# Second MLP weights prepared on GpSimd during the attention and kept in DRAM; sums of the first MLP weights on GpSimd; second-matmul tiles one product later

## The chip, the core and the metric

The kernel runs on one core of one Trainium2 chip. The metric is the time of one execution on the device in microseconds (us). Before the change it is 2522.59 us (median of three runs, 2522.47 to 2524.62).

Five things run side by side, each with a queue of its own that is worked off strictly in order: PE (TensorE, matmuls), DVE (VectorE), ACT (ScalarE), POOL (GpSimd) and SP (here only the issuer of DMA transfers). An instruction at the head of a queue that waits for another engine holds up all that stands behind it.

## The reference

One transformer block over 2048 tokens of width 576 in float32: attention with 32 heads of width 18 that share one key and value head, then a channel MLP of width 4608, both with modulated layer norms.

```
mod = (silu(c) @ w_mod) -> sa, ca, ga, sb, cb, gb
h = layernorm(x) * (1 + ca) + sa
x = x + ga * attention(h)                     # softmax, one k and v head for 32 q heads
h = layernorm(x) * (1 + cb) + sb
y = layernorm(h)                              # the MLP's own norm
x = x + gb * (gelu(y @ w1 + b1) @ w2 + b2)    # w1: 576x4608, w2: 4608x576
```

## The kernel before

**Precision.** Most large matmuls take operands in a rounded float32 form that PE reads in one pass. To keep accuracy an operand is split into a rounded part ("hi", written by ACT with a rounding copy) and a remainder ("lo", the difference, written by DVE or POOL), and a product of two operands is the three matmuls hi*hi, hi*lo and lo*hi.

**Three stages.** The first stage normalises the input and makes q, k and v. The second is the attention: 32 steps n (one per group of heads and block of 512 tokens), each with 16 inner steps kc. Between them `between` (L785) puts work of other kinds into the queues: `posts` finish a group of heads, and at every odd kc `step(fill)` takes one more piece of a generator (L803): output projection, the second layer norm of the first two token blocks (`ln2_tile`, L516, whose multiply and add are on POOL for these blocks), and at the last n `first_split` (L694), which splits the first group of first-MLP weights.

**The MLP stage** (L834 to L1067) is a loop over 36 steps v: two halves of 1024 tokens, 18 groups of 256 hidden columns. A step multiplies the normalised input, two blocks of 512 tokens by two column halves, with the group's first weights. It uses seven products (`product`, L909) in place of eight: sums and differences of input pieces (`op_pieces`) and of weight pieces (`w1_sum`, S1 to S4) are multiplied and the results combined. I call the products P1 to P7 in their order in the loop: three of six matmuls and four of eight. After P4, P5, P6 and P7 a 128-partition result of 512 columns goes through `gelu` (L924). I call these four gelus g00, g11, g10 and g01 after the f and b in the code. Each is a chain: two ACT operations on the result in PSUM (L931, L932), DVE (L934), ACT tanh (L935), DVE (L937), ACT hi (L938), POOL lo (L939). Its work buffer `gx` has two copies.

The result of step v goes into the second matmul, `fc2` (L941), which is a generator of eight tiles, T1 to T8 here, each 12 matmuls of 288 columns and one DVE addition into the residual `XT` (L958). These tiles run in step v+1, one per call of `t_()`, between the products. Their PSUM tile `psA` has two buffers, so a tile can start only after the DVE addition of the tile two before it.

**Weights.** The first weights of step v+1 are split during step v. The raw group (`w1r`, 640 KB) is loaded once per step into one buffer (L646, at the end of the step, issued by SP when the last reader of the old group is done). `w1_sum` (L665) makes a sum on DVE, ACT writes its hi (L649), and `w1_sum_lo` (L681) writes its lo on DVE (L652); single pieces have their lo on POOL (`w1_a`, `w1_22`, `w1_tails`). The second weights of a group (two pieces of 128x576) are loaded raw (L900) in every step, scaled with the gate `BC[:, 2]` on POOL (L905), rounded on ACT (L906) and their lo made on POOL (L907): `w2_split`. This happens twice per group, once for each half of the tokens.

**What else runs in the loop.** `more()` puts one piece of a generator at seven places of each step. In v = 1 to 9 this is the second layer norm of the last two token blocks, one tile of 128 tokens per step, with multiply and add on DVE (L534, L535). In v = 17 it forms the input pieces for the second half (`op_pieces`). I call the other steps (v = 10 to 16 and 18 to 34) the plain steps.

**Between attention and MLP** (L862 to L888) the input pieces of the first half are formed on ACT, DVE and POOL while PE ends the last output projection.

Of the kernel before, what the change touches and what calls it, by code (L numbers as in the profile page):

```python
# [8 lines left out]
F32 = mybir.dt.float32  # L9
# [23 lines left out]
def block_kernel(ctx: ExitStack, tc, x, wqkv, wo, w1, b1, w2, b2, c, wmod, ident_in, out):  # L33
# [31 lines left out]

    qscr = dr.tile([NB, 2, H * DH, TB], F32, name="qscr")
# [449 lines left out]
    def ln2_tile(tb, t):  # L516
# [17 lines left out]
        e.tensor_mul(h, h, BC[:, 1, :])  # L534
        e.tensor_tensor(h, h, BC[:, 0, :], op=ALU.add)  # L535
# [101 lines left out]
    def w1_rooms():  # L637
        W1["a"] = px.tile([128, KD, 2, 128], F32, name="w1r")
        W1["s"] = px.tile([128, 2, 128], F32, name="w1s")
        W1["d"] = px.tile([128, 128], F32, name="w1d")  # L640
# [24 lines left out]
    def w1_sum(a):  # L665

        o = W1["s"]
        def op(x, y, how):
            ve.tensor_tensor(o, x, y, op=how)  # L669
# [11 lines left out]
    def w1_sum_lo(a):  # L681
        w1_lo(a, 2, W1["s"], ve)

    def w1_tails(e=po):
# [3 lines left out]
        ve.tensor_tensor(d, t[:, 0], t[:, 1], op=ALU.subtract)  # L688
        ac.activation(W1["r"][:, 16], d, AF.Copy)
        for o, i in ((slice(14, 16), t), (16, d)):  # L690
            h = W1["r"][64:, o]
            e.tensor_tensor(h, i[64:], h.bitcast(F32), op=ALU.subtract)

    def first_split():  # L694
# [5 lines left out]
        w1_sum(4)  # L700
        w1_a()
        w1_sum_lo(4)
        yield
        w1_sum(6)
        w1_22()
        w1_sum_lo(6)
        yield
        w1_sum(10)
        w1_sum_lo(10)
        yield  # L710
        w1_sum(12)
        w1_sum_lo(12)
# [72 lines left out]
    def between(n, kc):  # L785
# [16 lines left out]
        if kc % 2:  # L802
            step(fill)  # L803

# [34 lines left out]
    def op_pieces(R):  # L839


        at = {"B11": (0, 0, ve), "B21": (2, 2, po), "B22": (4, 7, po), "T2": (6, 5, ve), "T1": (8, 5, ve),
              "T3": (10, 0, ve), "T4": (12, 2, ve), "t0": (0, 4, po), "t1": (1, 9, po)}
# [18 lines left out]
    form = op_pieces(YR[0])  # L862
# [5 lines left out]
    todo = deque(("+B11 +T2", "-B11 =T3 +B21 +T3", "-T2 -B21", "-T3"))  # L868
# [11 lines left out]
    form("+t0 -t0 =T4 =T1 +T1 +T4 +t1 -t1")  # L880
# [4 lines left out]
    form("-T1 -T4 +B22 -B22")  # L885
# [5 lines left out]
    W2R = [px.tile([128, D], F32, name="w2r", bufs=2) for _ in range(2)]  # L891
# [6 lines left out]
    def load_w2(v):  # L898
        for f in range(2):
            sy.dma_start(W2R[f], w2[v % NG, :, f, :])  # L900

    def w2_split(v, f, e):

        (h, l), o = W2[v % 2], W2R[f]
        e.tensor_tensor(o, o, BC[:, 2, :], op=ALU.mult)  # L905
        ac.activation(h[:, f], o, AF.Copy)  # L906
        e.tensor_tensor(l[:, f], o, h[:, f].bitcast(F32), op=ALU.subtract)  # L907
# [68 lines left out]
    load_w2(0)  # L976
    for v in range(NV):
        nx = v + 1 < NV
        e2 = po if v else ve
# [128 lines left out]
```

## Time and profile before

| what | value |
|---|---|
| median of three runs | 2522.59 us |
| profiled execution, its own time | 2520.07 us |
| its span, first to last instruction | 2518.3 us |
| mean granted PE clock | 0.987 |
| busy share PE, DVE, ACT, POOL | 93%, 83%, 71%, 36% |
| first MLP product starts at | 1447.24 us |

How to read it. The page gives busy time of each engine over the whole span, and in 40 equal slices a digit for the busy tenths. The windows view gives the same for stretches that one names. The groups view (lines) gives for each line, operation and shape the count, the busy time and the mean time of one. In the timeline a row is start, duration, engine, line, operation, output and inputs, and in brackets how long the engine had been idle before and what ended that. The chain of waits goes back from the last instruction to whatever released each step. PE's busy time contains the filling of its pipeline, so a busy PE isn't yet PE at its peak. A row "PE ... x12" that follows an idle time begins a tile.

### The profile page before, as it was taken

How to read it: one execution, taken by the hardware profiler on the slowest of the kernel's cores; microseconds unless marked ns; L12 is line 12 of the kernel's file. 1: busy time of each engine (PE TensorE's matmuls, PEld its weight loads, DVE VectorE, ACT ScalarE, POOL GpSimd, SP SyncE). 2: the span in 40 equal slices, each digit the busy share in tenths (PEclk: the TensorE clock that was granted, in tenths of full speed). 3: DMA queues.
4: the chain of work that ended last, by engine and by line, in shares of the span. 5: the costliest groups of instructions: out<-in, count | busy, mean ns of one | idle time of the engine just before them, and what ended most of it. 6: DMA issues, size and time to landing. Idle time of an engine off the chain costs nothing.

```text
span 2518.3 us, 43839 instructions
## 1 busy us (share of the span) xinstructions
PE 2351.6 (93%) x16586; PEld 1468.0 (58%) x16586; DVE 2080.7 (83%) x3644; ACT 1791.9 (71%) x3512; POOL 902.6 (36%) x860
## 2 busy tenths in 40 slices
PE   8999999999999999999999978888899798899898
PEld 6644444444444544445444467777788687788777
DVE  6689999889999899997999378877777777777776
ACT  5479999889999799997999844444545555545553
POOL 6513111132410233310110145555555555555554
PEclk9999999999999999999999989999999899999999
DMA  6421000000000000000000011111111121111111
GB/s 214 132 79 41 21 22 21 16 23 21 18 21 13 20 18 21 18 21 13 21 24 12 17 53 44 39 39 40 41 51 45 45 73 45 48 44 47 43 51 48
DMA packets 48229, 102.20 MB, mean 41 GB/s; under 512 B 6683, under 2 KB 10395, under 8 KB 48017
## 3 DMA queue, kind: packets, MB, share of 16 engines
q1 hardware_dynamic: 48017, 99.39, 12.9%
q8 instruction: 131, 2.15, 0.4%
q14 instruction: 81, 0.66, 0.1%
HBM read 76.32 MB, written 14.16 MB: 36 GB/s over the span
## 4 chain that ended last, share of the span: by engine, by line
PE 52%; ACT 15%; DVE 14%; POOL 10%; issue 7%; DMA 1%; SPq 0%; DVEq 0%; POOLq 0%; ACTq 0%
PE psC L750 19%; PE psB L761 10%; PE psM L312 9%; POOL w2r L905 4%; PE psB L771 4%; DVE gx L937 3%; ACT P L763 3%; DVE w1s L669 2%; ACT psB L935 2%; PE psB L241 2%; PE psA L954 2%; ACT gx L931 2%; PE psB L584 2%; ACT psB L932 2%; POOL big L939 2%
## 5 line engine op out<-in xcount | busy, mean ns | idle before, releaser
L763 ACT ACTIVATE P<-psB 128x512 f32<-128x512 f32 x2048 | 1050.6, 621 | 1.5 <-PE psB L761 0.6
L783 DVE TENSOR_REDUCE mx<-psM 128x1 f32<-128x512 f32 x1476 | 943.5, 683 | 56.2 <-PE psM L312 29.6
L954 PE MATMUL psA<-w2s,big 128*128 128x288 f32 x2880 | 529.8, 304 | 113.4 <-DVE XT L958 86.5
L750 PE MATMUL psC<-P,V 128*32 128x256 f32 (+1 forms) x6056 | 598.0, 466 | 13.0 <-ACT O L603 13.0
L761 PE MATMUL psB<-qst,KS 64*128 64x512 f32 x2048 | 598.2, 433 | 0.5 <-DMA qst<-ms 0.4
L312 PE MATMUL psM<-KS,qst 64*128 64x512 f32 x1722 | 594.4, 431 | 2.1 <-DVE mx L783 2.1
L954 PEld LDWEIGHTS psA<-w2s,big 128*128 128x128 f32 x2880 | 445.9, 193 | 160.3 <-DVE XT L958 56.5
L919 PE MATMUL psB<-ops,w1a 128*128 128x512 f32 x1512 | 401.6, 402 | 8.4 <-DVE psB L1029 5.1
L761 PEld LDWEIGHTS psB<-qst,KS 64*128 64x128 f32 x2048 | 305.3, 184 | 168.4 <-issue 72.5
L312 PEld LDWEIGHTS psM<-KS,qst 64*128 64x128 f32 x1722 | 284.0, 184 | 121.8 <-DVE mx L781 82.5
L939 POOL TENSOR_TENSOR big<-gx,big 128x512 fp32r<-128x512 f32 x144 | 194.9, 1354 | 332.9 <-ACT big L938 198.9
L919 PEld LDWEIGHTS psB<-ops,w1a 128*128 128x128 f32 x1512 | 276.2, 192 | 57.9 <-DVE psB L1029 5.7
L750 PEld LDWEIGHTS psC<-P,V 128*32 128x32 f32 x6056 | 119.6, 108 | 231.2 <-issue 207.6
L958 DVE TENSOR_TENSOR XT<-psA,XT 128x576 f32<-128x576 f32 x288 | 212.4, 748 | 26.7 <-PE psA L954 26.6
L774 ACT ACTIVATE xc<-psB 128x512 f32<-128x512 f32 x246 | 148.2, 602 | 90.4 <-PE psM L312 75.3
L938 ACT ACTIVATE big<-gx 128x512 fp32r<-128x512 f32 x144 | 90.9, 631 | 160.1 <-DVE gx L937 160.1
L354 POOL CAST ms<-mf 16x128 fp32r<-16x128 f32 x32 | 9.0, 282 | 542.8 <-ACT mf L353 542.8
L906 ACT ACTIVATE w2s<-w2r 128x576 fp32r<-128x576 f32 x72 | 49.4, 686 | 205.1 <-POOL w2r L905 200.3
L652 DVE TENSOR_TENSOR w1a<-w1s,w1a 128x256 fp32r<-128x256 f32 x144 | 103.2, 717 | 100.2 <-ACT w1a L649 88.7
L954 PE MATMUL psA<-w1a,big 128*128 128x288 f32 x576 | 171.5, 298 | 0.0
L781 DVE CUSTOM_DVE_ANT_0 xc<-psM,xc 128x512 f32<-128x512 f32 x246 | 167.3, 680 | 0.0
L935 ACT ACTIVATE psB<-gs 128x512 f32<-128x512 f32 x144 | 86.1, 598 | 109.4 <-DVE gs L934 109.4
(167 smaller groups left out, 2810.4 us busy)
## 6 DMA issues: line engine op xcount, KB each, us to landing
w1r<-in_w SPq DMA_DIRECT2D x36, 640.0 KB
w2r<-in_w SPq DMA_DIRECT2D x72, 288.0 KB
qst<-qscr SPq DMA_DIRECT2D x192, 72.0 KB
qscr<-qs SPq DMA_DIRECT2D x16, 504.0 KB
big<-os SPq DMA_DIRECT2D x112, 72.0 KB
bigw<-in_wmod SPq DMA_DIRECT2D x5, 1440.0 KB
out<-XT SPq DMA_DIRECT2D x16, 288.0 KB
XT<-in_x SPq DMA_DIRECT2D x3, 1152.0 KB
```

What stands on the lines that cost most here:

```text
L312: pe.matmul(o, QST[n][64 * g:64 * g + 64, p, 128 * qt:128 * (qt + 1)], KS[64 * g:64 * g + 64, 512 * kb:512 * (kb + 1)], start=True, stop=True)
L750: pe.matmul(PVt[n][32 * j:32 * (j + 1), cs], V[:, kc, :], t[:, j, cs], start=(kc == 0 and h0 == 0), stop=(kc == 15), skip_group_check=True)
L761: pe.matmul(t, KS[64 * g:64 * g + 64, 128 * kc:128 * (kc + 1)], QST[n][64 * g:64 * g + 64, i, :], start=True, stop=True)
L763: ac.activation(P[n, kc][:, 2 * i + g, :], t, AF.Exp, scale=SCALE)
L774: ac.activation(XC[-1], t, AF.Relu)
L781: ve.tensor_tensor_reduce(c, t, c, 1.0, -3.0e38, ALU.add, ALU.max, o)
L783: ve.tensor_reduce(o, t, axis=AX.X, op=ALU.max)
L919: pe.matmul(o, x, y, start=(first and i == 0), stop=(i == len(terms) - 1), skip_group_check=True)
L935: ac.activation(p, s, AF.Tanh, scale=GC * GA3)
L939: po.tensor_tensor(GT[:, 2 * u + 1], h, GT[:, 2 * u].bitcast(F32), op=ALU.subtract)
L954: pe.matmul(p[:, nn, :288], x, y, start=(q == 0), stop=(q == len(terms) - 1))
L958: ve.tensor_tensor(Xv, p[:, :, :288], Xv, op=ALU.add)
```

## The change

Four edits, all quoted in the diff below.

1. **Second weights in the attention.** A generator `w2_parts` runs in the attention from n = 3 on, one piece at every odd kc after `step(fill)`. For each of the 36 pieces of 128x576 it loads the raw weights (SP), scales them, rounds them and makes the lo (three POOL operations), and stores hi and lo in DRAM (`w2scr`). Four pieces of the generator make one weight piece, so two weight pieces fall on one n, and it ends at n = 20. Its tiles share the buffers `w1s` and `w1r` that `first_split` uses later. In the MLP `w2_split` is gone, and `load_w2` brings hi and lo ready from DRAM, two transfers of 576 KB per step, at the start of step v, where raw transfers of 288 KB came in the middle of the step before.
2. **Sums on GpSimd.** In the MLP `w1_sum`, `w1_sum_lo` and the difference in `w1_tails` go to POOL; in `first_split` the sums stay on DVE. The multiply and add of `ln2_tile` are on POOL for all four token blocks.
3. **Second-matmul tiles one product later.** T1 comes after P2 (in v = 1 after P3), T2 after P3, T3 after P4, T4 after P5, T5 and T6 after P6, T7 and T8 after P7.
4. **Input pieces at the start.** Of the pieces of the first half, the lo parts of B21, B22, t0 and t1 go from POOL to DVE; T4 and T1 are formed after the last additions of the output projection; the lo parts of T1, t1, T4 and B22 are made inside step v = 0.

```
+    w2scr = dr.tile([NG, 128, 2, 2, D], F32, name="w2scr")
...
-        e.tensor_mul(h, h, BC[:, 1, :])
-        e.tensor_tensor(h, h, BC[:, 0, :], op=ALU.add)
+        po.tensor_mul(h, h, BC[:, 1, :])
+        po.tensor_tensor(h, h, BC[:, 0, :], op=ALU.add)
...
-    def w1_sum(a):
+    def w1_sum(a, e=po):
...
-            ve.tensor_tensor(o, x, y, op=how)
+            e.tensor_tensor(o, x, y, op=how)
...
-    def w1_sum_lo(a):
-        w1_lo(a, 2, W1["s"], ve)
+    def w1_sum_lo(a, e=po):
+        w1_lo(a, 2, W1["s"], e)
...
-        ve.tensor_tensor(d, t[:, 0], t[:, 1], op=ALU.subtract)
+        e.tensor_tensor(d, t[:, 0], t[:, 1], op=ALU.subtract)
...
+    def w2_parts():
+
+        for g in range(NG):
+            for f in range(2):
+                o = px.tile([128, D], F32, name="w2o", tag="w1s")
+                sy.dma_start(o, w2[g, :, f, :])
+                yield
+                po.tensor_tensor(o, o, BC[:, 2, :], op=ALU.mult)
+                yield
+                hl = px.tile([128, 2, D], F32R, name="w2p", tag="w1r")
+                po.tensor_copy(hl[:, 0], o)
+                yield
+                po.tensor_tensor(hl[:, 1], o, hl[:, 0].bitcast(F32), op=ALU.subtract)
+                sy.dma_start(w2scr[g, :, :, f, :], hl.bitcast(F32))
+                yield
...
         if kc % 2:
             step(fill)
+            if n > 2:
+                step(prep)
...
-    todo = deque(("+B11 +T2", "-B11 =T3 +B21 +T3", "-T2 -B21", "-T3"))
+    todo = deque(("+B11 +T2", "-B11 =T3 +B21 +T3", "-T2 -T3", "-B21"))
...
-    form("+t0 -t0 =T4 =T1 +T1 +T4 +t1 -t1")
+    form("+t0 -t0")
...
-    form("-T1 -T4 +B22 -B22")
+    form("=T4 =T1 +T1 +t1 +T4 +B22")
...
     def load_w2(v):
-        for f in range(2):
-            sy.dma_start(W2R[f], w2[v % NG, :, f, :])
-
-    def w2_split(v, f, e):
-
-        (h, l), o = W2[v % 2], W2R[f]
-        e.tensor_tensor(o, o, BC[:, 2, :], op=ALU.mult)
-        ac.activation(h[:, f], o, AF.Copy)
-        e.tensor_tensor(l[:, f], o, h[:, f].bitcast(F32), op=ALU.subtract)
+        for l in range(2):
+            sy.dma_start(W2[v % 2][l].bitcast(F32), w2scr[v % NG, :, l])
...
+        load_w2(v)
         ba = psB()
         product(ba, 0, 0)
         ac.activation(U[:, 0], ba, AF.Copy)
-        t_()
         g_()
...
-        t_()
-        g_()
-        w2_split(v, 0, e2)
+        if v != 1:
+            t_()
+        g_()
...
-        more("-T2 =T3")
+        more("-T2 =T3", "-T1 -t1")
         t_()
+        if v == 1:
+            t_()
...
-        w2_split(v, 1, e2)
         if nx:
             w1_sum_lo(6)
-            load_w2(v + 1)
...
         g_()
+        t_()
         product(bd, 12, 4, False, (2, 1))
```

The next two excerpts of the instruction order show a plain step. First POOL before the change, one step from the lo of g10 on (`big<-gx`, the gelu's lo). L692 are the tail pieces of the first weights, L905 and L907 the scaling and the lo of the second weights, L652 the lo of single first-weight pieces.

```order
L939 TENSOR_TENSOR big<-gx,big 128x512
L692 TENSOR_TENSOR w1a<-w1r,w1a 64x256
L692 TENSOR_TENSOR w1a<-w1d,w1a 64x128
L939 TENSOR_TENSOR big<-gx,big 128x512
L905 TENSOR_TENSOR w2r<-w2r,BC 128x576
L907 TENSOR_TENSOR w2s<-w2r,w2s 128x576
L652 TENSOR_TENSOR w1a<-w1r,w1a 128x512
```

The same place on POOL after it, again from the lo of g10 on: L672 are the additions that make a sum, L691 the difference of the tails, L695 the tail pieces (L692 before), L655 the lo of sums and of pieces, L954 the gelu's lo.

```order
L954 TENSOR_TENSOR big<-gx,big 128x512
L672 TENSOR_TENSOR w1s<-w1r,w1a 128x256
L672 TENSOR_TENSOR w1s<-w1s,w1a 128x256
L691 TENSOR_TENSOR w1s<-w1r 128x128
L695 TENSOR_TENSOR w1a<-w1r,w1a 64x256
L695 TENSOR_TENSOR w1a<-w1s,w1a 64x128
L655 TENSOR_TENSOR w1a<-w1s,w1a 128x256
L954 TENSOR_TENSOR big<-gx,big 128x512
L672 TENSOR_TENSOR w1s<-w1r 128x256
L672 TENSOR_TENSOR w1s<-w1s,w1r 128x256
L655 TENSOR_TENSOR w1a<-w1s,w1a 128x256
L655 TENSOR_TENSOR w1a<-w1r,w1a 128x512
```

The scaling and lo of the second weights are gone from this queue. In their place stand the additions of S4 and, behind the lo of g01, those of S2, whose first operand is the freshly loaded `w1r`.

On DVE before, the end of a step and the start of the next one (L1051 is the addition behind P7, L958 the addition of a second-matmul tile, L669 an addition for a sum, L688 the difference of the tails):

```order
L1051 TENSOR_TENSOR psB<-psB,u 128x512
L937 SCALAR_TENSOR_TENSOR gx<-psB,gx 128x512
L958 TENSOR_TENSOR XT<-psA,XT 128x576
L669 TENSOR_TENSOR w1s<-w1r,w1a 128x256
L669 TENSOR_TENSOR w1s<-w1s,w1a 128x256
L688 TENSOR_TENSOR w1d<-w1r 128x128
L652 TENSOR_TENSOR w1a<-w1s,w1a 128x256
L958 TENSOR_TENSOR XT<-psA,XT 128x576 x2
L934 SCALAR_TENSOR_TENSOR gs<-psB,gx 128x512
```

The same place on DVE after (L1067 was L1051, L973 was L958, L952 and L949 were L937 and L934):

```order
L973 TENSOR_TENSOR XT<-psA,XT 128x576
L1067 TENSOR_TENSOR psB<-psB,u 128x512
L952 SCALAR_TENSOR_TENSOR gx<-psB,gx 128x512
L973 TENSOR_TENSOR XT<-psA,XT 128x576 x2
L949 SCALAR_TENSOR_TENSOR gs<-psB,gx 128x512
```

The four weight operations between the tile additions are gone, and every DVE instruction left here has one operand in PSUM.

44 lines of the change are left out of this document (23 added, 21 removed).

## The prediction

> **What bounds the kernel now.** I began with the page.
>
> ```profile
> span 2518.3 us, 43839 instructions
> PE 2351.6 (93%) x16586; PEld 1468.0 (58%) x16586; DVE 2080.7 (83%) x3644; ACT 1791.9 (71%) x3512; POOL 902.6 (36%) x860
> PE   8999999999999999999999978888899798899898
> ```
>
> PE is full in the middle, which is the attention, and falls to 8 and 7 in the last 17 slices. The windows view gives this by stage: window, length, PE, PEld, DVE, ACT, POOL, granted clock, DMA.
>
> ```profile
> 300.00:1157.00 857.00, 846.17 (x7079) 372.72 (x7079) 785.00 (x1525) 791.88 (x1583) 197.29 (x211) 1.00 0.07 19
> 1512.00:1775.60 263.60, 224.71 (x1239) 194.92 (x1238) 215.34 (x348) 117.18 (x225) 144.31 (x135) 0.95 0.13 41
> 2039.83:2206.80 166.97, 150.73 (x877) 132.39 (x876) 127.41 (x192) 84.30 (x162) 87.76 (x73) 1.00 0.15 46
> ```
>
> The attention has PE at 846 of 857 us: nothing is to be had there, and POOL has 660 us free. The other two rows are MLP steps with and without the layer norm. The steps are read off the chain of waits, in which the second-weight scaling L905 recurs once or twice per step.
>
> ```profile
> 1518.20 1.93 POOL w2r L905
> 1775.60 1.59 POOL w2r L905
> 1942.46 1.59 POOL w2r L905
> 2039.83 1.58 POOL w2r L905
> 2457.17 1.60 POOL w2r L905
> 2479.81 1.58 PE psA L954 x12
> ```
>
> These L905 rows are the first of v = 2, 10, 16, 19 and 34. The plain step is (2457.17 - 2039.83) / 15 = 27.82 us, and (1942.46 - 1775.60) / 6 = 27.81 confirms it. A step with the layer norm is (1775.60 - 1518.20) / 8 = 32.2. Three steps from 1942.46 to 2039.83 take 97.4, so v = 17 takes 97.4 - 2 x 27.8 = 41.7. What PE needs for a step, and where it waits, is in the timeline of one plain step.
>
> ```profile
> 2040.93 1.76 PE L954 MATMUL psA<-w2s,big 128*128 128x288 f32 x12
> 2044.40 1.75 PE L954 MATMUL psA<-w2s,big 128*128 128x288 f32 x12
> 2054.42 1.85 PE L954 MATMUL psA<-w2s,big 128*128 128x288 f32 x12 [1.37 <-DVE XT L958]
> 2058.39 1.40 POOL L939 TENSOR_TENSOR big<-gx,big 128x512 fp32r<-128x512 f32 x1 [1.75 <-ACT big L938]
> 2058.46 0.37 PE L954 MATMUL psA<-w2s,big 128*128 128x288 f32 x1 [0.79 <-DVE XT L958]
> 2058.68 1.39 DVE L669 TENSOR_TENSOR w1s<-w1s,w1a 128x256 f32<-128x256 f32 x1
> 2059.84 0.54 PE L954 MATMUL psA<-w2s,big 128*128 128x288 f32 x2 [0.47 <-POOL big L939]
> 2060.88 1.57 PE L919 MATMUL psB<-ops,w1a 128*128 128x512 f32 x6
> 2063.87 1.56 PE L919 MATMUL psB<-ops,w1a 128*128 128x512 f32 x6
> ```
>
> A tile and a product of eight matmuls take 2044.40 - 2040.93 = 3.47 us, a tile and a product of six 2063.87 - 2060.88 = 2.99, a tile alone 1.58 (2479.81 above). PE's need is 4 x 3.47 + 3 x 2.99 + 1.58 = 24.4 us. So 3.4 us of a plain step are waits, and they all lie around T8 and T1: T8 waits 1.37 for the buffer that DVE's addition L958 frees, T1 0.79 for the same and 0.47 for the gelu's lo from POOL. DVE is late there because it is held up, not because it is full (127 of 167 us): the addition L669 at 2058.68 takes 1.39 us, and ends 0.28 behind the POOL instruction that began at 2058.39. DVE operations with one operand in PSUM aren't held up so (L958 below).
>
> **The change: plain steps (24 of 36).** These groups of the same window carry durations.
>
> ```profile
> L958 DVE TENSOR_TENSOR XT<-psA,XT 128x576 f32<-128x576 f32 x48 | 35.4, 749 | 2.9 <-PE psA L954 2.9
> L939 POOL TENSOR_TENSOR big<-gx,big 128x512 fp32r<-128x512 f32 x24 | 32.1, 1339 | 57.9 <-ACT big L938 33.5 <-issue 24.4
> L905 POOL TENSOR_TENSOR w2r<-w2r,BC 128x576 f32<-128x576 f32 x13 | 21.0, 1618 | 0.0
> L652 DVE TENSOR_TENSOR w1a<-w1s,w1a 128x256 fp32r<-128x256 f32 x24 | 18.9, 788 | 18.1 <-ACT w1a L649 18.1
> L937 DVE SCALAR_TENSOR_TENSOR gx<-psB,gx 128x512 f32<-128x512 f32 x24 | 16.5, 689 | 10.0 <-ACT psB L935 8.4
> L938 ACT ACTIVATE big<-gx 128x512 fp32r<-128x512 f32 x24 | 15.1, 631 | 25.9 <-DVE gx L937 25.9
> L935 ACT ACTIVATE psB<-gs 128x512 f32<-128x512 f32 x24 | 14.4, 598 | 17.7 <-DVE gs L934 17.7
> L649 ACT ACTIVATE w1a<-w1s 128x256 fp32r<-128x256 f32 x24 | 9.9, 413 | 6.1 <-DVE w1s L669 6.1
> L669 DVE TENSOR_TENSOR w1s<-w1r 128x256 f32<-128x256 f32 x18 | 9.1, 504 | 0.9 <-DMA w1r<-in_w 0.7
> L907 POOL TENSOR_TENSOR w2s<-w2r,w2s 128x576 fp32r<-128x576 f32 x6 | 8.6, 1433 | 4.8 <-ACT w2s L906 4.8
> L652 POOL TENSOR_TENSOR w1a<-w1r,w1a 128x256 fp32r<-128x256 f32 x6 | 4.4, 740 | 1.0 <-ACT w1a L649 1.0
> ```
>
> POOL loses 2 x (1.62 + 1.43) = 6.1 us per step and ACT two roundings. POOL gains six additions and four lo of 128x256 at 0.74, and a difference, 7.9 us. It is busy for some 16.5 of 27.8 us then, less than DVE was, and DVE keeps eight tile additions, eight gelu operations and five additions behind P2, P3 and P5 to P7, some 15 us. No engine is full. But the sums now stand in POOL's queue, their hi in ACT's queue ahead of the gelus', so one chain runs through all engines. I follow it from the first addition of S2 (time 0), with handoffs of 0.1. An ACT or DVE operation lets the next one start 0.05 to 0.1 before its end.
>
> Two additions for S2 on POOL, 1.5. ACT: hi of S2, the two operations of g00 behind it, hi of the four first pieces: to 3.6 (some 0.35, 0.6, 0.6 and 0.6). POOL: their lo 1.34 (128x512, as L939) and the addition of S3 0.74: 5.7. ACT: hi of S3, then tanh of g00 0.60: 6.65. DVE 0.69, ACT hi 0.63, POOL lo 1.3: 9.45. POOL addition for S1 0.74, ACT hi, tanh of g11: 11.1. DVE 0.69, ACT hi 0.63, two operations of g10, DVE: 14.5. The tile addition of T6 and the one behind P7 stand before g10's last DVE operation: 0.7 + 0.6 + 0.69, 16.4. ACT hi, POOL lo: 18.45. POOL: two additions for S4, the difference, first tail piece 0.74: 21.45. Now the raw weights are free, and SP loads the next ones; S2 of the next step waits for them. The load's price:
>
> ```profile
> 2201.08 0.33 SPq L646 DMA_DIRECT2D w1r<-in_w  x1
> 2206.16 0.91 DVE L669 TENSOR_TENSOR w1s<-w1r 128x256 f32<-128x256 f32 x1 [0.72 <-DMA w1r<-in_w]
> 2061.79 0.33 SPq L646 DMA_DIRECT2D w1r<-in_w  x1
> 2066.08 0.42 DVE L669 TENSOR_TENSOR w1s<-w1r 128x256 f32<-128x256 f32 x1
> ```
>
> One load lands 5.1 us after its issue; the other one is there before 4.3, since its sum didn't wait. I take 4.1, near the second, because only a single sum in the window waited (0.7 in the L669 group). The chain closes at 21.45 + 4.1 = 25.55. A side chain gives as much: S4's hi on ACT delays the copy behind P1, and over it g01's lo, which stands before S2 in POOL's queue, to some 25.5. On this chain PE has slack, since 25.5 is above 24.4; T7 and T8 wait together some 1.1. With a little for jitter I take 25.6: 24 x (27.8 - 25.6) = 53 us. Bounds: 24.6 (PE nearly full), -77; 27.4 (loads at 5.1, additions at 0.85, as L905 takes 1.62 where L907 takes 1.43), -10.
>
> The Trainium skill, GPSIMD Engine Reference, section Engine selection, speaks against this edit: elementwise work belongs on VectorE, GpSimd being about half as fast with two inputs. The clean DVE row at 2066.08 (0.42) against POOL's 0.74 agrees; by that rule ten operations cost 10 x 0.32 = 3.2 us more per step, 115 us over the kernel if POOL set the pace. The rows hold the other half: on DVE the same operations took 0.79 (L652) and 1.39 where POOL was busy, and POOL has room.
>
> **Steps with the layer norm (v = 1 to 9).** Today 4.4 us over a plain step. Two operations of 128x576 leave DVE for POOL at 1.43 each, in the same queue as the chain, but no longer held up on DVE. I keep 4.4: 30.0, a gain of 9 x 2.2 = 20. Bounds: none (the 2.9 us all on the chain, 32.4) and 9 x 5 = 45 (PE sets the pace at 24.4, some 1.5 for transposes, a little waiting).
>
> **The start, v = 17, the end.** In v = 0 PE waits 4.35 us for DVE, and in v = 1 T1 waits for the first gelus with P2 behind it:
>
> ```profile
> 1462.90 2.25 PE L919 MATMUL psB<-ops,w1a 128*128 128x512 f32 x6 [4.35 <-DVE psB L1029]
> 1474.26 2.05 PE L954 MATMUL psA<-w2s,big 128*128 128x288 f32 x7 [0.61 <-POOL big L939]
> ```
>
> In v = 0 DVE gets four lo of pieces but loses the second weights and sums: I expect P7 no earlier. In v = 1 P2 and P3 move into T1's wait: two products, 2 x 1.4, and T1 up to 2 us sooner: -5 (0 to -10). v = 17 loses the second weights on POOL but gets the sums behind large lo there: -2 (+3 to -8). The last step has no sums: nothing.
>
> **The attention** gets 36 x (1.62 + about 1 + 1.43) = 146 us of POOL in n = 3 to 20, with 36 loads and stores. PE's dependence on POOL there is the row maximum: POOL splits it and SP sends it to the query tile, today with a wait of 0.4 us in all (the page's row of L761). DVE's transposes there aren't slower beside POOL:
>
> ```profile
> L761 PE MATMUL psB<-qst,KS 64*128 64x512 f32 x2048 | 598.2, 433 | 0.5 <-DMA qst<-ms 0.4
> L607 DVE STREAM_TRANSPOSE T<-O x32: 699/701/712, 184.6 to 1431.4; 128x512 f32<-128x512 f32 x32
> ```
>
> Two weight pieces fill the eight odd kc of one n, so at kc = 13 always the rounding follows, in POOL's queue behind the split of the maximum, and the scaling comes two kc earlier, at kc = 11: 5 us (32 transposes L607 from 184.6 to 1431.4 are 40.2 us per n, 2.5 per kc). The cover is this alignment; without it up to 1.6 us per n, 18 x 1.6 = 29 us. I take +2, bounds 0 and +29.
>
> Sum: -53 - 20 - 5 - 2 + 2 = -78 against the profiled execution's own 2520.07, so 2442. The three runs' median lies 2.5 higher, at 2522.59; I say 2443.
>
> **Rivals.**
>
> *PE sets the pace.* If the chain is shorter than I count, the plain step is 24.6 and that with the norm 27.5: -24 x 3.2 - 9 x 4.7 - 7 = -126, 2396. For it: only the sequence of waits keeps PE from 24.4. Against it: two chains close at 25.5. Chance 0.15.
>
> *GpSimd's additions eat the gain.* The plain step ends at 27.4, the norm steps stay: -10 - 5 = -15, 2507, and with 0.4 us more per step there is no change. For it: L905 shows that POOL can take 13% longer, and six additions are on the chain. Against it: the 740 ns row has the same size. It decides where the additions take over 1.0 us. Chance 0.14. The Trainium skill's rule above is this mechanism.
>
> *The raw load queues with the second weights, and it gets slower.* SP now issues two transfers of 576 KB right behind the 640 KB of `w1r`. If all three share the DMA engines evenly, the load ends with the last, after 1.79 MB in place of 0.64: 7.8 us if half of the 4.1 is fixed, 11.5 if nothing is. I take 9.0: the plain step is 21.45 + 9.0 = 30.4, 2.6 over today, and with as much in the steps with the norm 24 x 2.6 + 9 x 2.6 - 7 + 2 = +81, 2601. It decides from 6.4 us on, where the chain passes 27.8. For it: the trace has no load with so much behind it. Against it: all are issued by SP, one after another. The Trainium skill, DMA: Bandwidth & Descriptors, section Queues, rings and completion order, says that a DMA engine takes the descriptors of a ring in order, which would leave the load at its 4.1; no run here shows that so far. Chance 0.07.
>
> *The attention loses its alignment:* +29 there, 2472, still faster. Chance 0.04.
>
> **The numbers.** My forecast has 0.60: 2443, from 2415 to 2475 by the ends that are likely together. The range of 2400 to 2496 adds the attention's loss, a part of the GpSimd rival and a part of PE's. A difference under 0.2% (5 us) can't be told from none. Slower: the load, and 0.01 for what I don't see, 0.08. Within 0.2%: the GpSimd rival's upper end, 0.05. Faster: 0.87.
>
> **What would show it.** In the after profile: the plain step (from one tile row to the same one of the next step) 25.6 us; PE's waits at T7 and T8 and not at T1; additions for sums on POOL 0.74; S2 waiting on the load of `w1r`, landing 4.1 us after its issue; the steps with the norm 30; in 300 to 1157 PE as busy as now. Wrong would be: a plain step of 24.5 or over 27, a landing over 6 us, or an attention longer by over 5 us.

## The result, and the profile after

The changed kernel takes 2455.72 us (median of four runs, 2453.26 to 2461.99). The kernel before takes 2523.49 beside it (four runs, 2522.47 to 2524.62). The ratio is 0.9735 [0.9716, 0.9754], so 68 us are gained. The profiled execution took 2455.7 with a span of 2453.8, which is 64.5 less span than before. Two lines of the page answer to those of before.

```profile
PE 2331.5 (95%) x16586; PEld 1459.2 (59%) x16586; DVE 1807.8 (74%) x3242; ACT 1741.5 (71%) x3440; POOL 1089.4 (44%) x1226
PE   8999999999999999999999996988899899999999
```

DVE has fallen from 83% to 74% and POOL has risen from 36% to 44%. The last eight slices of PE are 9 now; before, four of them were 8.

The load of the raw first weights `w1r` is issued once per step, when the last reader of the old group is done. So it marks the end of a step. In these rows of SP's timeline, first of before, the marks are the first load in the attention, the ends of v = 0, v = 1, v = 9 and v = 18, and the last load, at the end of v = 33.

```profile
1393.62 0.44 SPq L646 DMA_DIRECT2D w1r<-in_w  x1
...
1475.40 0.33 SPq L646 DMA_DIRECT2D w1r<-in_w  x1
1511.60 0.33 SPq L646 DMA_DIRECT2D w1r<-in_w  x1
...
1769.75 0.33 SPq L646 DMA_DIRECT2D w1r<-in_w  x1
...
2034.36 0.49 SPq L646 DMA_DIRECT2D w1r<-in_w  x1
...
2451.29 0.33 SPq L646 DMA_DIRECT2D w1r<-in_w  x1
```

The same marks of after:

```profile
1397.58 0.44 SPq L649 DMA_DIRECT2D w1r<-in_w  x1
...
1479.32 0.33 SPq L649 DMA_DIRECT2D w1r<-in_w  x1
1517.94 0.33 SPq L649 DMA_DIRECT2D w1r<-in_w  x1
...
1758.84 0.33 SPq L649 DMA_DIRECT2D w1r<-in_w  x1
...
2004.35 0.34 SPq L649 DMA_DIRECT2D w1r<-in_w  x1
...
2390.79 0.33 SPq L649 DMA_DIRECT2D w1r<-in_w  x1
```

The differences between neighbouring marks give where the time went. The column "forecast" holds the prediction's terms, cut to the same stretches. The marks at the ends of v = 16 and v = 17 are at 1964.45 and 2006.62 before, and at 1938.75 and 1976.74 after.

| stretch | before | after | difference | forecast |
|---|---|---|---|---|
| up to the first load (first stage, attention) | 1393.6 | 1397.6 | +4.0 | +2 |
| v = 0 (from the second load on) | 28.6 | 28.5 | -0.1 | -5, with v = 1 |
| v = 1 | 36.2 | 38.6 | +2.4 | -2.2 |
| v = 2 to 9 | 258.2 | 240.9 | -17.3 | -17.6 |
| v = 10 to 16 | 194.7 | 179.9 | -14.8 | -15.4 |
| v = 17 | 42.2 | 38.0 | -4.2 | -2 |
| v = 18 | 27.7 | 27.6 | -0.1 | -2.2 |
| v = 19 to 33 | 416.9 | 386.4 | -30.5 | -33.0 |
| v = 34 and the end | 67.0 | 63.0 | -4.0 | -2.2 |
| sum | | | -64.5 | -77.6 |

A plain step is 386.44 / 15 = 25.76 us, where it was 27.80. What sets this length is shown by the chain of waits, from the last load (at the end of v = 33) to the gelu that follows S1's sum (start, duration, what):

```profile
2390.79 3.89 DMA w1r<-in_w
...
2394.81 0.74 POOL w1s L672
...
2395.63 0.75 POOL w1s L672
...
2396.72 0.68 ACT gx L946
2397.40 0.55 ACT psB L947
2397.94 0.56 ACT w1a L652
...
2398.57 1.30 POOL w1a L655
2399.86 0.71 POOL w1s L672
...
2403.04 1.29 POOL big L954
2404.34 0.70 POOL w1s L672
...
2406.08 0.70 DVE gx L952
```

This is the loop that the prediction counted through: the load, S2's sums on POOL (L672), g00's two ACT operations, the hi and the lo of the first pieces (L652, L655), S3's sum, the gelu's lo (L954), S1's sum, the next gelu. From there the chain of the last step follows PE to the end, so the rest of the loop is read from the timeline of the step before: S2's first sum, g10's lo, which waits for ACT, the tail piece, and PE's wait at T7.

```profile
2369.23 0.74 POOL L672 TENSOR_TENSOR w1s<-w1r 128x256 f32<-128x256 f32 x1 [0.35 <-DMA w1r<-in_w]
...
2384.45 1.85 PE L969 MATMUL psA<-w2s,big 128*128 128x288 f32 x12 [0.72 <-DVE XT L973]
...
2386.34 1.29 POOL L954 TENSOR_TENSOR big<-gx,big 128x512 fp32r<-128x512 f32 x1 [2.19 <-ACT big L953]
...
2390.02 0.74 POOL L695 TENSOR_TENSOR w1a<-w1r,w1a 64x256 fp32r<-64x256 f32 x1 [0.48 <-POOL w1s L691]
```

The next load is issued at 2390.79, right behind this piece. From S2's first sum to the end of the piece are 21.53 us, where the prediction counted 21.45.

The load landed in 3.89 us, with 1.15 MB of second weights issued behind it on the same queue. This puts out the rival that lets the load share with what is behind it. The Trainium skill, DMA: Bandwidth & Descriptors, section Queues, rings and completion order, says that a DMA engine takes a ring's descriptors in order. The row agrees.

The windows view of v = 19 to 33 has POOL at 240 us of 386, so POOL isn't full:

```profile
2004.35:2390.79 386.44, 372.64 (x2192) 330.54 (x2191) 211.49 (x316) 189.71 (x376) 240.00 (x286) 1.00 0.20 72
```

A group of the same stretch and PE's waits in it give the prices. First the group.

```profile
L672 POOL TENSOR_TENSOR w1s<-w1r 128x256 f32<-128x256 f32 x45 | 33.1, 736 | 5.8 <-DMA w1r<-in_w 5.6
```

The waits of PE (us in total, times, longest):

```profile
PE psA L969 <- DVE XT L973: 13.6, 22, 0.8
```

A sum takes 0.74 us, as forecast, and PE waits 13.6 / 15 = 0.9 us per step, where 1.1 was forecast. POOL's wait for the load is 5.6 us in 15 steps, 0.4 per step. In the rest of those 3.9 us POOL makes S4's lo, waits for g01's gelu and makes its lo, which is the prediction's side chain.

### The profile page after: what moved, and what is told of

The parts are those of the page before. It is cut to its first block, busy times and chain, and to the rows that moved or that the text cites. A ratio compares the mean times of both kernels' runs of the same rounds, so it can differ in the third digit from the quotient of the medians.

```text
span 2453.8 us, 43998 instructions
## 1 busy us (share of the span) xinstructions
PE 2331.5 (95%) x16586; PEld 1459.2 (59%) x16586; DVE 1807.8 (74%) x3242; ACT 1741.5 (71%) x3440; POOL 1089.4 (44%) x1226
## 5 line engine op out<-in xcount | busy, mean ns | idle before, releaser
L969 PE MATMUL psA<-w2s,big 128*128 128x288 f32 x2880 | 510.9, 300 | 60.9 <-DVE XT L973 60.5
L969 PEld LDWEIGHTS psA<-w2s,big 128*128 128x128 f32 x2880 | 437.4, 191 | 94.2 <-DVE XT L973 81.7
L934 PE MATMUL psB<-ops,w1a 128*128 128x512 f32 x1512 | 395.8, 401 | 17.1 <-ACT yr L160 10.5
L934 PEld LDWEIGHTS psB<-ops,w1a 128*128 128x128 f32 x1512 | 275.6, 191 | 70.2 <-ACT yr L160 11.9
L973 DVE TENSOR_TENSOR XT<-psA,XT 128x576 f32<-128x576 f32 x288 | 215.5, 750 | 105.2 <-PE psA L969 103.1
L954 POOL TENSOR_TENSOR big<-gx,big 128x512 fp32r<-128x512 f32 x144 | 187.3, 1300 | 228.2 <-ACT big L953 219.7
L652 ACT ACTIVATE w1a<-w1s 128x256 fp32r<-128x256 f32 x144 | 60.6, 421 | 319.1 <-POOL w1s L672 313.2
L949 DVE SCALAR_TENSOR_TENSOR gs<-psB,gx 128x512 f32<-128x512 f32 x144 | 99.4, 690 | 100.1 <-ACT psB L947 99.6
L952 DVE SCALAR_TENSOR_TENSOR gx<-psB,gx 128x512 f32<-128x512 f32 x144 | 98.9, 687 | 89.7 <-ACT psB L950 89.4
```

The source lines that it names most:

```text
L934: pe.matmul(o, x, y, start=(first and i == 0), stop=(i == len(terms) - 1), skip_group_check=True)
L949: ve.scalar_tensor_tensor(s, p, 1.0 / GA3, h, op0=ALU.add, op1=ALU.mult)
L954: po.tensor_tensor(GT[:, 2 * u + 1], h, GT[:, 2 * u].bitcast(F32), op=ALU.subtract)
L969: pe.matmul(p[:, nn, :288], x, y, start=(q == 0), stop=(q == len(terms) - 1))
L973: ve.tensor_tensor(Xv, p[:, :, :288], Xv, op=ALU.add)
```

## The experiments

The table has all runs. Each ratio is against runs of the kernel before on the same chip, whose median was 2523.49 for the change and 2520.75 to 2521.45 for the others. "LN" is the mean of v = 2 to 9, "plain" the mean of v = 19 to 33, both from the marks of SP's timeline (for e6, whose loads stand elsewhere, v = 19 to 32). The steps are each from one profiled execution.

| run | us | ratio | v = 0 | v = 1 | LN | plain |
|---|---|---|---|---|---|---|
| before | | | 28.6 | 36.2 | 32.3 | 27.80 |
| after | 2455.72 | 0.9735 [0.9716, 0.9754] | 28.5 | 38.6 | 30.1 | 25.76 |
| e3_noshift | 2448.04 | 0.9709 [0.9696, 0.9723] | 29.3 | 37.5 | 29.5 | 25.63 |
| e2_s2late | 2450.05 | 0.9718 [0.9705, 0.9731] | 29.2 | 38.6 | 31.0 | 25.06 |
| e6_raw2 | 2448.40 | 0.9712 [0.9699, 0.9725] | 28.8 | 39.8 | 29.8 | 25.38 |
| e1_b2g | 2445.43 | 0.9701 [0.9688, 0.9714] | 31.0 | 29.0 | 29.7 | 25.66 |
| e7_even | 2449.08 | 0.9719 [0.9703, 0.9735] | 29.9 | 38.8 | 30.6 | 25.60 |
| e8_best | 2437.43 | 0.9668 [0.9655, 0.9681] | 30.7 | 30.0 | 31.2 | 25.03 |
| e10_w2back | 2630.18 | 1.0432 [1.0417, 1.0446] | 32.7 | 39.5 | 36.0 | 30.68 |
| e4_dve | 2415.31 | 0.9581 [0.9568, 0.9594] | 28.3 | 39.5 | 28.9 | 24.58 |
| e5_dve_noshift | 2430.34 | 0.9644 [0.9631, 0.9657] | 28.3 | 37.9 | 28.7 | 25.34 |
| e11_dve_b2g_even | 2404.91 | 0.9540 [0.9527, 0.9553] | 28.4 | 30.3 | 28.9 | 24.54 |
| e12_lnve | 2399.85 | 0.9521 [0.9508, 0.9534] | 28.3 | 28.8 | 28.3 | 24.56 |
| e13_oldstart | 2399.21 | 0.9514 [0.9501, 0.9527] | 26.4 | 28.6 | 28.3 | 24.54 |

### Is it the loop? e3_noshift, e2_s2late, e6_raw2

**e3_noshift** undoes edit 3 alone: the tiles stand where they stood before.

```
         ac.activation(U[:, 0], ba, AF.Copy)
+        t_()
         g_()
...
-        if v != 1:
-            t_()
+        t_()
         g_()
...
-        if v == 1:
-            t_()
...
         g_()
-        t_()
         product(bd, 12, 4, False, (2, 1))
```

> Only the shift of the second-matmul tiles is undone (T1 again behind P1). If the loop sets the pace, T1 is ready by then and TensorE has slack: plain steps 25.8 to 26.0, 2455 to 2462. If the shift took away the waits at T1, these come back, about 1.2 us per plain step: 2485 or more.

Measured: 2448.04, a plain step of 25.63, both a little under the range for the loop. So the shift gains nothing here; if anything it costs, by 0.0026 of the ratio, which is about as much as the noise of the two. In this run the loop's length doesn't depend on where PE's tiles stand.

**e2_s2late** puts S2's sums and lo behind the first operations of g00, which so leave the loop: ACT can do them while the load is under way.

```
-        if nx:
-            w1_sum(4)
         more("-T2 =T3", "-T1 -t1")
...
-        if nx:
-            w1_sum_lo(4)
         product(ba, 2, 2, False, (0, 0))
...
         if nx:
+            w1_sum(4)
+            w1_sum_lo(4)
             w1_a()
```

> The sum S2 and its rounding are moved behind the first two operations of gelu g00, so that these no longer stand behind S2 in ScalarE's queue. If the loop through GpSimd, ScalarE and the load of the first weights sets the pace, it loses about 1.1 us: plain steps 24.7 us in place of 25.76, 2428 in all. If TensorE with its two result buffers, or the busy time of GpSimd, sets the pace: plain steps as before, 2456.

Measured: 2450.05, a plain step of 25.06. That is between what the two theories gave. The chain of waits of this run says why the loop became only 0.7 us shorter:

```profile
2312.75 0.74 POOL w1s L672
2313.49 0.49 issue
...
2314.01 1.99 POOL w1a L655 x2
```

The two ACT operations of g00 (1.23 us in after's chain) are gone from between the sums and the lo, but S2's hi and lo have come into the line: POOL idles 0.49 us for the hi, and then makes two lo in a row (1.99 us, where after has one of 1.30 at this place). In the steps with the norm the move loses (31.0 for 30.1). So the order in the queues sets the plain step here, and I had counted the new order too short. For the whole kernel the gain isn't clear of noise.

**e6_raw2** takes the load out of the loop: two buffers for the raw weights, loaded one step ahead.

```
-        W1["a"] = px.tile([128, KD, 2, 128], F32, name="w1r")
+        if not W1.get("a"):
+            W1["a"] = px.tile([128, KD, 2, 128], F32, name="w1r")
...
+    RAW = deque()
+    def load_raw(i):
+        RAW.append(px.tile([128, KD, 2, 128], F32, name="w1q", bufs=2))
+        sy.dma_start(RAW[-1].rearrange("p k f c -> p k (f c)"), w1[i])
...
+        if v + 2 < NV:
+            load_raw((v + 2) % NG)
         load_w2(v)
+        if nx:
+            W1["a"] = RAW.popleft()
...
-        if v + 2 < NV:
-            load_w1((v + 2) % NG)
```

> The raw first weights get two buffers and are loaded at the start of a step, so the sum S2 never waits for its load. If the load closes the loop alone: plain steps near 24.4 to 24.6 us, 2425. If, as counted, the side chain over g01's lo closes at nearly the same time: plain steps 25.4 to 25.6, 2448 to 2453. A wait elsewhere: 2456.

Measured: 2448.40, a plain step of 25.38, as expected for the side chain. The 3.9 us of the load are gone from the loop, and the step is 0.4 us shorter, as much as POOL had waited for the load. In the chain of waits of this run g01's lo (L961) stands right before S2's first sum, and no load:

```profile
2105.25 1.29 POOL big L961
2106.54 0.70 POOL w1s L673
```

So the side chain that the prediction put at 25.5, over g01's lo in POOL's queue, is real and nearly as long. That two closed loops are almost equally long fits with how little single edits gain here.

### Where the start went: e1_b2g

In v = 1 a tile waits 16.0 us for its buffer. The timeline of after shows what it waits for (in brackets the idle time before and what ended it):

```profile
1479.69 0.43 SPq L922 DMA_DIRECT2D w2s<-w2scr  x1
1480.17 0.43 SPq L922 DMA_DIRECT2D w1a<-w2scr  x1
1480.71 0.51 SPq L562 DMA_DIRECT2D b2g<-in_b  x1
1487.03 1.40 POOL L563 TENSOR_TENSOR b2g<-b2g,BC 128x576 f32<-128x576 f32 x1 [6.50 <-DMA b2g<-in_b]
1491.07 1.51 DVE L533 TENSOR_SCALAR Z<-XT,mv,rs 128x576 f32<-128x576 f32 x1 [10.63 <-POOL rs L145]
...
1496.54 1.37 DVE L973 TENSOR_TENSOR XT<-psA,XT 128x576 f32<-128x576 f32 x2
1497.30 1.09 PE L969 MATMUL psA<-w2s,big 128*128 128x288 f32 x3 [15.99 <-DVE XT L973]
```

The same load before:

```profile
1475.82 0.94 SPq L561 DMA_DIRECT2D b2g<-in_b  x1
...
1480.34 1.43 POOL L562 TENSOR_TENSOR b2g<-b2g,BC 128x576 f32<-128x576 f32 x1 [4.54 <-DMA b2g<-in_b]
```

The load of the second bias, `b2g`, is issued behind the raw weights (1479.32) and both transfers of second weights. POOL stands still for it until 1487.03, 6.3 us after its issue. Before, only `w1r` stood ahead of it, and it took 4.5 us. Counted from the mark at which the step begins, the bias reaches POOL after 7.7 us, where it was 4.9, so the new place on SP's queue makes it 2.8 us later. Behind it in POOL's queue is `rs`, for which DVE waits 10.63 us, and behind that wait in DVE's queue are the additions of T1 and T2 (1496.54), which free PE's buffers. Before, T1 and T2 came earlier in the step: their additions ran at 1476.34 and 1479.87, ahead of the norm's scaling on DVE at 1484.42. e1_b2g loads and scales the bias ahead of the loop, which takes the load and its two POOL operations out of v = 1 together:

```
-    B2.clear()
+    b2g = B2["b"] = px.tile([128, D], F32, name="b2g")
+    sy.dma_start(b2g, b2.to_broadcast([128, D]))
+    po.tensor_mul(b2g, b2g, BC[:, 2, :])
+    po.tensor_scalar(b2g, b2g, 2.0, None, op0=ALU.mult)
```

> Step v = 1 of the changed kernel takes 38.6 us, because the load of the second bias is issued behind both second-weight transfers and everything on GpSimd waits 6.5 us for it. Here that load and its two GpSimd operations come before the loop, where GpSimd waits for the first weights anyway. If the queue in front of the load is the cause: v = 1 near 30 us, 2447 in all. If the layer norm's own chain is the cause: less than 2 us won, 2454 or more.

Measured: 2445.43, near the time expected for the first case. v = 1 falls from 38.6 to 29.0 us. Its wait for a tile buffer in v = 1 is

```profile
PE psA L972 <- DVE XT L976: 6.3, 1, 6.3
```

where it was 16.0. v = 0 is 2.5 us longer in this run, which I didn't follow up. In both steps together 7.1 us come back, so that they are 4.8 us shorter than before the change, where 7.2 was forecast. The run prices the bias in v = 1 as a whole. It doesn't say how much of that is the later load and how much the load and its two operations, which stood in v = 1 before the change too.

### The attention: e7_even

The first load comes 4 us later than before. By DVE's reciprocal, of which there is one per n, two of the 32 steps hold nearly all of it, n = 11 (+2.45 us) and n = 19 (+1.39). There pieces of the layer norm and of the preparation meet on POOL. In the timeline of after, in one of these steps, a lo of the preparation (L709) stands in POOL's queue ahead of the norm's operations and of POOL's multiplication, DVE's transpose waits for the multiplication (1.65 us, where it was 0.25 before), the row maximum stands behind that transpose in DVE's queue, and PE waits for the row maximum:

```profile
587.68 1.42 POOL L709 TENSOR_TENSOR w2p<-w2o,w2p 128x576 fp32r<-128x576 f32 x1
...
596.50 1.05 POOL L612 TENSOR_TENSOR T<-T,R 128x512 f32<-128x512 f32 x1
597.58 0.71 DVE L614 STREAM_TRANSPOSE O<-T 128x512 f32<-128x512 f32 x1 [1.65 <-POOL T L612]
599.28 0.76 PE L313 MATMUL psM<-KS,qst 64*128 64x512 f32 x1 [1.80 <-DVE mx L804]
```

e7_even moves the preparation to the even kc.

```
             step(fill)
-            if n > 2:
-                step(prep)
+        elif n > 2:
+            step(prep)
```

> The preparation steps stand at even kc, away from the layer norm's pieces. If the attention's 4 us come from GpSimd being late for the multiplication between the two transposes, behind layer-norm pieces and preparation of the same kc: first MLP weights reach the chip 3 to 4 us earlier, 2452. If they come from the transfers or the mere load on GpSimd: no change, 2456.

Measured: 2449.08 (2447.30 to 2457.01; the profiled execution took 2456.85), not clear of the change. The two jumps are gone (-0.02 and -0.05 us at these n), but two of 1.17 and 1.13 us come at the steps behind them, with some of 0.6 to 1.2 elsewhere. The first load is at 1397.1, for 1397.6, and not 3 to 4 us earlier. Runs whose attention is the change's own put it anywhere from 1397.3 to 1401.6, the five runs with the even kc from 1395.1 to 1399.8, and the two without preparation at 1392.7 and 1393.6. So the preparation costs some 4 to 9 us there, the place of the waits is shown by the rows, and whether the even kc are better stays open.

### All three together: e8_best

e8_best holds the edits of e1, e2 and e7 at once.

> Early bias load, S2 behind g00 and preparation at even kc together. If the three effects add up: 2456 less 8, 28 and 3, about 2417. If they share one limit: 2428 or more.

Measured: 2437.43, 0.9668, far from the faster of the two times. The plain step of 25.03 is that of e2 alone (25.06), so the loop goes on setting it. The single gains over the change, by the ratios 0.34%, 0.17% and 0.16%, add up to the 0.67% that came, but the first is uncertain by more than half of its size, and the other two aren't clear of noise.

### What the prepared second weights are worth: e10_w2back

This run undoes edit 1 alone: POOL scales and splits the second weights in every step again, with the sums on POOL as well.

```
-    prep = deque([w2_parts()])
+    prep = deque()
...
-        for l in range(2):
-            sy.dma_start(W2[v % 2][l].bitcast(F32), w2scr[v % NG, :, l])
+        for f in range(2):
+            sy.dma_start(W2R[f], w2[v % NG, :, f, :])
+    def w2_split(v, f, e):
+        (h, l), o = W2[v % 2], W2R[f]
+        e.tensor_tensor(o, o, BC[:, 2, :], op=ALU.mult)
+        ac.activation(h[:, f], o, AF.Copy)
+        e.tensor_tensor(l[:, f], o, h[:, f].bitcast(F32), op=ALU.subtract)
...
         g_()
+        w2_split(v, 0, e2)
...
+        w2_split(v, 1, e2)
         if nx:
             w1_sum_lo(6)
+            load_w2(v + 1)
```

> Only the preparation of the second weights is undone: scaling, rounding and lo are in the MLP again, in the places where they were. If GpSimd's queue is on the loop, each of the two splits (1.6, 0.7 and 1.4 us in sequence) lengthens it by 2 to 4 us: plain steps 30 to 32, 2560 to 2620. If they fill GpSimd's idle time: plain steps at most 27, 2490 or less; the attention is 4 us shorter in both cases.

Measured: 2630.18, 4.3% slower than before and 10 us above the range for a loop through POOL, with a plain step of 30.68. Two POOL groups of its v = 19 to 33 (of the lo, about half write to another tile and are a group of their own):

```profile
L926 POOL TENSOR_TENSOR w2r<-w2r,BC 128x576 f32<-128x576 f32 x30 | 42.5, 1416 | 0.0
L928 POOL TENSOR_TENSOR w2s<-w2r,w2s 128x576 fp32r<-128x576 f32 x14 | 19.9, 1418 | 11.1 <-ACT w2s L927 11.1
```

Four such operations of 1.42 us are 5.7 us per step, and the step is 30.68 - 25.76 = 4.9 us longer. PE is slower there too: its granted clock in these steps is 0.94, where it is 1.00 in the change, and it is busy 1.5 us longer per step for the same matmuls. Whether that adds to the step isn't shown. The run doesn't say what edit 1 is worth with the sums on DVE. That follows from e5 below.

### What the sums on GpSimd are worth: e4_dve, e5_dve_noshift

**e4_dve** keeps the change, but sums, their lo and the tail difference go back to DVE.

```
-    def w1_sum(a, e=po):
+    def w1_sum(a, e=ve):
...
-    def w1_sum_lo(a, e=po):
+    def w1_sum_lo(a, e=ve):
...
-        e.tensor_tensor(d, t[:, 0], t[:, 1], op=ALU.subtract)
+        ve.tensor_tensor(d, t[:, 0], t[:, 1], op=ALU.subtract)
```

> Only the sums, their lo and the tail difference are back on VectorE. If the loop sets the pace, six additions in it become 0.3 us shorter but wait for GpSimd's port now and then: plain steps 24.5 to 26.5, 2425 to 2475. If freeing VectorE was what the change lived from: plain steps over 27, 2490 or more.

Measured: 2415.31, 0.9581 [0.9568, 0.9594], 39 us faster than the change (0.0154 of 2521), and 10 us under the range that I gave. The plain step is 24.58. The chain of waits in a plain step of this run (2200 to 2226), summed by engine and line, has no engine but PE:

```profile
by line: PE psA L969 55.3%; PE psB L934 44.9%
```

So PE sets the pace, at what the prediction had put as its need (24.4). DVE is still held up by POOL, as the timeline of a plain step of this run shows:

```profile
2104.17 1.40 POOL L954 TENSOR_TENSOR big<-gx,big 128x512 fp32r<-128x512 f32 x1 [2.17 <-PE psA L969]
2104.45 1.40 DVE L672 TENSOR_TENSOR w1s<-w1s,w1a 128x256 f32<-128x256 f32 x1
...
2112.36 0.43 DVE L672 TENSOR_TENSOR w1s<-w1s,w1r 128x256 f32<-128x256 f32 x1
```

The addition beside the POOL instruction takes 1.40 us and ends 0.28 behind it, one of the same shape alone takes 0.43. But this costs DVE time that it has, and PE hardly waits for DVE: 0.5 us in v = 19 to 33.

**e5_dve_noshift** has the edits of e4 and of e3: prepared second weights, norm on POOL, the new start, but sums on DVE and the tiles as before.

```
-    def w1_sum(a, e=po):
+    def w1_sum(a, e=ve):
...
         ac.activation(U[:, 0], ba, AF.Copy)
+        t_()
         g_()
...
```

> Sums on VectorE and T1 again behind P1: of the MLP loop's edits only the prepared second weights (and the layer norm's two operations on GpSimd) are left. If GpSimd's splits were what made the gelus and T1 late, the shift isn't needed: plain steps 24.6 to 25.0 us, 2415 to 2425. If T1's wait belongs to the gelus' own chain, it comes back: 25.6 or more, 2440.

Measured: 2430.34, a plain step of 25.34, between the two cases and nearer to the second. PE's waits in 14 plain steps:

```profile
PE psA L969 <- POOL big L954: 7.3, 14, 0.5
```

T1 waits once per step for the gelu's lo, 0.5 us, as before the change. The shift removes it: 25.34 - 24.58 = 0.76 us per plain step, and 16 us by the ratios of e5 and e4. With the sums on POOL the same shift was worth nothing (e3). This is the ladder of the change: the second weights with the norm and the start bring 90 us (0.9644), the shift 16 more (0.9581), and the sums on POOL give 39 back (0.9735).

In a plain step e5 differs from the kernel before by edit 1 alone, and 27.80 - 25.34 = 2.46 us are gone, of the 3.4 that PE waited. DVE's sums are still held up in it (window 2100 to 2239; the same group of before has a mean of 1385 ns):

```profile
L672 DVE TENSOR_TENSOR w1s<-w1s,w1a 128x256 f32<-128x256 f32 x6 | 8.3, 1383 | 0.2
```

So most of the waits at T8 and T1 came with the second weights in the step and not from the sums on DVE.

### The rest, one part at a time: e11, e12, e13

**e11_dve_b2g_even** is e4 with the bias ahead of the loop and the preparation at the even kc (both diffs above).

> Sums on VectorE, early bias load, preparation at even kc. If the three are independent: 2415 less 10 (v = 1) and 2 to 4 (attention), 2402. If v = 1 or the attention are held by something else, 2410 or more.

Measured: 2404.91, v = 1 at 30.3 us for 39.5 in e4. That is 3 us above the sum of three independent gains. The early bias is clear in v = 1; the even kc aren't (first load at 1397.6, for 1400.2 in e4).

**e12_lnve** puts the multiply and the add of the norm back on DVE for the last two blocks:

```
-        po.tensor_mul(h, h, BC[:, 1, :])
-        po.tensor_tensor(h, h, BC[:, 0, :], op=ALU.add)
+        e.tensor_mul(h, h, BC[:, 1, :])
+        e.tensor_tensor(h, h, BC[:, 0, :], op=ALU.add)
```

> As the kernel with sums on VectorE, early bias load and even kc, with multiply and add of the last two blocks' layer norm on VectorE again. If VectorE is the later one in those steps: each of the nine gets 0.5 to 2 us longer, 2407 to 2420. If GpSimd's wait chain is: 2395 to 2400.

Measured: 2399.85, as expected for GpSimd's wait chain. A step with the norm is 28.3 for 28.85, and v = 1 is 1.6 us shorter. By the marks that is 8 x 0.54 + 1.6 = 5.9 us (5 by the ratios, about the size of their noise), so with the sums on DVE this part of edit 2 cost time as well.

**e13_oldstart** undoes edit 4 on top of that:

```
-    form = op_pieces(YR[0], ve)
+    form = op_pieces(YR[0], po)
...
-    form("+t0 -t0")
+    form("+t0 -t0 =T4 =T1 +T1 +T4 +t1 -t1")
...
-    form("=T4 =T1 +T1 +t1 +T4 +B22")
+    form("-T1 -T4 +B22 -B22")
...
-        more("-T2 =T3", "-T1 -t1")
+        more("-T2 =T3")
...
```

> As the fastest kernel so far (sums and layer norm on VectorE, early bias load, even kc), with the input pieces at the start formed as before the change. If forming T1, t1, T4 and B22 inside v = 0 gains nothing, because TensorE waits for VectorE there either way: v = 0 within 1.5 us of 28.3, 2398 to 2402. If it does gain what the start was forecast to gain: 3 to 6 us longer, 2403 to 2406.

Measured: 2399.21. v = 0 is 26.4 for 28.3 us, a little more than the 1.5 us allowed for and the other way than a gain of edit 4, and the whole is the same within its interval. In this version edit 4 gains nothing. e12 and e13 can't be told apart, and both are the fastest versions here, 0.9521 and 0.9514 of before, 2.2% below the change. The windows view of e13 for v = 19 to 33 (length, PE, PEld, DVE, ACT, POOL, granted clock, DMA) is

```profile
1967.94:2336.02 368.08, 368.08 (x2189) 331.18 (x2188) 298.31 (x481) 193.60 (x375) 126.68 (x121) 1.00 0.21 77
```

PE is busy all the time there, so no wait of PE is left to be taken out of the plain steps. Whether another order of PE's own matmuls would fill its pipeline better wasn't tried.

## Why the prediction was right, and where not

The forecast was 2443 us, 80 us under the time before; 2455.72, 68 us under, was measured, inside the range that was given. The span missed by 13 us.

**Plain steps: right in mechanism and nearly in size.** The loop is in the chain of waits and the timeline with the forecast's members, 21.53 us for 21.45 from S2 to the tail piece, and e6 shows the side chain. A step is 25.76 and not 25.6, which makes 2.4 us of v = 19 to 33. Another 2.1 are v = 18, the first step of the second half, which I had counted as a plain one: it stayed at 27.6. PE waits 2.5 us there for tile buffers, about as much as before (2.6 in all). What holds DVE there stays open.

**Steps with the norm: right in size.** 2.16 us per step in v = 2 to 9, for 2.2. That POOL's two operations lie on the path, which the prediction left between its bounds, is shown by e12 for the version with the sums on DVE; in the change itself it wasn't tried.

**The start: wrong.** The step that failed is "In v = 1 P2 and P3 move into T1's wait ... -5". v = 0 and v = 1 together were to give 7.2 us and cost 2.4, which is 9.5 of the 13 us by which the forecast missed the span. The term looked at PE and the gelus and not at what stands ahead of the tile additions in DVE's queue: there PE waits 16.0 us in one piece for T1's and T2's additions, which stand behind the norm's scaling, which waits for `rs` on POOL, which stands behind the bias. The longest wait of PE in v = 1 was 4.2 us before. The move of `load_w2` to the start of a step was billed for `w1r`, ahead of which nothing comes, and not for what stands behind it in SP's queue; that makes the bias 2.8 us later. e1 shows that the bias as a whole is worth 9.6 us in v = 1, and 7.1 with v = 0. How the miss divides between the later bias, the later tiles and the norm's operations on POOL wasn't separated; undoing the later tiles alone (e3) brings v = 1 from 38.6 to 37.5 only.

**v = 17 and the end** gave 4.2 and 4.0 us for 2 and 2.2. I don't know why; by luck these 4 us cover a part of what the other terms missed.

**The attention: a cost of the forecast's kind, at another place.** +4.0 for +2. The cover named there held: the wait on the way of the row maximum to the query tile is 0.3 us in all. But DVE's transposes wait for POOL's multiplication where the norm's pieces and the preparation meet, and no term was made for that.

**Why DVE was late before: put down to the wrong thing in the main.** The prediction read the 3.4 us of waits as DVE being held up in its sums by POOL. The hold-up is there, but e5 keeps it, and 2.46 us of the waits are gone with edit 1. The shift takes 0.76 us more (e4 against e5). Neither needs the sums on POOL.

**The sums on POOL.** The prediction weighed them by the price of one operation, 0.74 for 0.42 us, and answered that POOL has room. POOL has room indeed (240 of 386 us), and the prices are as said, but room wasn't the question. With the sums on POOL a loop through all queues takes 25.76 us, where PE needs 24.58, and e4 puts the difference at 39 us over the kernel. The prediction's own figures had it: a loop of 25.55 beside a need of 24.4. I took that as the result and didn't ask what the same steps would be without edit 2. How much of the 39 us is the higher price of the sums on that loop (by an estimate from the rows, six additions at 0.3 us more each, 1.8 us per step, which alone would be enough) and how much their place in POOL's queue, no run separates. The Trainium skill, GPSIMD Engine Reference, section Engine selection, gives elementwise work to VectorE. e4 agrees, with 39 us and not with the 115 that the prices alone would make.

**The rivals.** PE doesn't set the pace in the change. It does so in e4. The additions on POOL take 0.74 and not over 1.0, so that rival is out as it was put. The raw load is out by its 3.89 us. The attention didn't lose its alignment: it took 4.0 us more and not 29.

## What to carry to other kernels

Work that is moved to an engine with room can make a loop through in-order queues longer than the need of the engine that should set the pace: add up that loop with the work in either place and hold it against that need, whatever the busy shares say. A moved transfer is billed on its queue in both directions, also for a small load that now stands behind it, in the one step that has such a load. Parts of a change are undone one at a time, and again after another part has gone: the shift was worth nothing with the sums on POOL and 16 us with them on DVE. That an engine is seen to be held up doesn't make the hold-up the cause of a wait: e5 left the hold-up in place, took something else away, and most of the wait was gone.

## What the runs showed of the hardware

- A DVE addition of 128x256 with all its operands in SBUF took 1.40 us beside POOL and 0.43 alone. In e4 PE waited for DVE only 0.5 us in 15 steps, so the hold-up was no reason by itself to move work to POOL.
- A load of 288 KB (one row of 576 values spread over 128 partitions) took 4.5 us from its issue behind one of 640 KB, and 6.3 us behind that and two of 576 KB. The 640 KB at the head landed in 3.9 us with the two of 576 KB behind it (4.4 in e2).
- The end of an attention of the same code varied by 4.3 us between builds that differ only in the MLP (1397.3 to 1401.6, one profiled execution of each, so whether the build or the execution makes it isn't known). This is as large as the effects that e7 was to tell apart.
